# Step 1 of a convolution-and-GELU kernel: taking the first needed sum and its copy ahead of the middle channel group

## The chip, the cores and the metric

The kernel runs on one core of one Trainium2 chip. The metric is the device time of one launch in microseconds, the median of the runs shown. TensorE (PE in the profile) multiplies matrices, VectorE (DVE), ScalarE (ACT) and GpSimd (POOL) work on elements, and SyncE (SP) issues most of the DMA transfers from an in-order queue.

## The reference

```python
# x: (8, 4096, 192), weight: (8 heads, 7 taps); w_in: (192, 2048), w_out: (2048, 192)
w = softmax(weight, axis=-1)
out[b, s, h, :] = sum_k w[h, k] * x_pad[b, s + k, h, :]     # causal, 6 zeros ahead of s = 0
h = out.reshape(32768, 192) @ w_in                          # float32
g = h * sigmoid(1.702 * h)
y = g @ w_out
```

A depthwise causal convolution over 7 positions feeds a two-layer network whose hidden layer has 2048 columns. All is float32.

## The kernel before, in words

The 32768 tokens are taken in 32 steps (`big` 0 to 31). A step covers two halves of tokens at a time, and its input is turned so that channels lie on partitions. The 192 channels are three groups (`c` = 0, 1, 2) of 64, and each group gives two blocks of 256 positions: group 0 gives C11 and C12, group 1 gives C21 and C22, group 2 gives C31 and C32. A convolution of one group is seven instructions over 512 elements: the first tap is a multiplication (line 490), the other six are multiply-and-add on DVE (line 492). In step 1 the multiplication is on ACT (`times = act.mul`), in the later steps the group 0 taps run on ACT and POOL.

From step 1 on, the first matrix product is not done block by block: it uses 21 products (`TERMS`) of sums of blocks (`SUMS_C`, V1 to V8) with sums of weight blocks (`SUMS_W`). V1 is C31 - C11, so it needs groups 2 and 0 and nothing of group 1; V2 to V8 follow from it and the other blocks. A product (`product1`, line 570) runs on two halves of the partitions, and one half of each needs the block moved to the other 64 partitions. That is `cross`: two SP DMAs (line 514) from the step's own slab of `conv_t` into its middle slab. It is called three times a step: for V1 alone (2 x 64 KB), for C11 to C22 (2 x 256 KB), and for the remaining eight blocks (2 x 512 KB), V4 among them.

The order of DVE's work around the change is written as a list of (label, cost, action), made by `prepare`. `work(us)` takes actions off the front of that list as long as their costs fit the given time; `need(label)` takes all up to the label at once. `cross_when` issues a copy at once if the space that it writes is given free, and in step 1 it is free by the time that the list gets there.

Step 0 does its second matrix product in `second_first` (PE lines 739 and 745), four 32-column products at a time. While PE is in it, DVE does that stage's sums (lines 755 to 778) and the list of step 1 through `work(1.5)`, `work(5.0)`, `work(4.0)`. Then `fetch()`, which is `between` for this step, empties the list (`need("all 1")`), turns the input of step 2 (line 469), and issues step 1's first product, `terms(1, 0, slots[2], 16)`, which is V1 with a weight block. PE goes on with line 739 for the rest of step 0 and ends it with `rows22`; then `hidden(1, 0)` begins step 1 with `pe(sums, 12)`, V4 with a weight block, and `pe(x, 5, 17)`, C11 and C21.

```python
        work(4.0)
        go(c12, listed(s4, b22) + rows12[:cut], first=False)
        fetch()
        go(c21, listed(a22, b21), first=False)
        work(3.0)
        turn(1, 0, blocks(whole(c21)), js)
```

`add_forms` lets POOL issue accumulating DMAs (line 437, 240 KB each) that make sums of the second layer's weights at the same time.

Of the kernel before, what the change touches and what calls it, by code (L numbers as in the profile page):

```python
# [15 lines left out]
def kernel(  # L16
# [32 lines left out]
    H, K = weight.shape  # L49
# [31 lines left out]
    vec, act = nc.vector, nc.scalar  # L81
# [91 lines left out]
    def place(big, b):  # L173

        if b == V1:
            return V8 if big % 2 else C31
        return C31 if b == V8 and big % 2 else b

    def own(big):
        return conv_t[:, big % 2 * 2, :, :]  # L180
# [301 lines left out]
    def conv_src(big, c, k, ns=slice(0, 2)):  # L482
        return xts[big][:, c, ns, Q - PAD + k : Q - PAD + k + T]

    def conv(big, c, k, ns=slice(0, 2), times=vec.tensor_scalar_mul):
        src = conv_src(big, c, k, ns)
        dst = own(big)[:, 2 * c + ns.start : 2 * c + ns.stop, :]
        tap = cw[:, c, k : k + 1]
        if k == 0:
            times(dst, src, tap)  # L490
        else:
            vec.scalar_tensor_tensor(  # L492
                out=dst, in0=src, scalar=tap, in1=dst, op0=ALU.mult, op1=ALU.add
            )
# [10 lines left out]
    def sums_c(big, i):  # L505
        add_up(
            lambda j: own(big)[:, place(big, j), :],
            *SUMS_C[i],
            eng=vec if big == 1 else nc.gpsimd,
        )  # L510

    def cross(big, b0, b1):
        for o in range(2):
            nc.sync.dma_start(
                out=conv_t[halves[1 - o], 1, b0:b1, :], in_=own(big)[halves[o], b0:b1, :]
            )
# [11 lines left out]
    def cross_when(early, *what):  # L528
        if given[early] < what[0] - 1:
            waiting[early].append(what)  # L530
        else:
            cross(*what)
# [7 lines left out]
    def prepare(big):  # L540

        v1 = place(big, V1)
        for c in (2, 1, 0) if big == 1 else (2, 1):
            for k in range(K):
                times = act.mul if big == 1 else vec.tensor_scalar_mul
                yield "", 0.76 if k else 0.48, lambda c=c, k=k, times=times: conv(big, c, k, times=times)
        yield f"done {big}", 0.0, lambda: need(f"taps {big}")
        cost = 0.34 if big == 1 else 0.0
        yield "", cost, lambda: sums_c(big, 0)
        yield f"first {big}", 0.0, lambda: cross_when(True, big, v1, v1 + 1)  # L550
        yield "", 0.0, lambda: cross_when(False, big, 0, C31)
        for i in range(1, len(SUMS_C)):
            yield "", cost, lambda i=i: sums_c(big, i)
        rest = (C31, V8) if big % 2 else (C31 + 1, NB)
        yield f"all {big}", 0.0, lambda: cross_when(False, big, *rest)
# [430 lines left out]
    def need(label):  # L986
        for q in (todo, ready):
            while any(item[0] == label for item in q):
                q.pop(0)[2]()
# [30 lines left out]
    def first_step(fetch):  # L1020
# [81 lines left out]
        def stage_2():  # L1102
            round_w_out(0)
            load_w_out(3)
            todo.append(("", 2.1, lambda: turn_x(1)))
            todo.extend(prepare(1))
# [23 lines left out]
        def between():  # L1130
            need("all 1")
            turn_x(2)
            todo.extend(prepare(2))
            todo.append(("forms", 0.0, lambda: begin_forms(TURN_O)))
            fetch()
# [10 lines left out]
    def begin(big):  # L1146
        todo.extend(prepare(big))
        ready.extend(prepare_taps(big))
# [54 lines left out]
```

## Time and profile before

| what | value |
|---|---|
| median of 3 runs | 2319.04 us (2319.0 to 2319.4) |
| the profiled execution's own time | 2319.26 us |
| its span, first to last instruction | 2317.5 us |
| PE busy | 2306.4 us (100% of the span) |
| DVE, ACT, POOL busy | 2006.3 us, 1377.4 us, 432.8 us |
| chain that ended last, by engine | PE 98%, DVE 1% |
| PE line 570, products of the first layer into `slot` | 3740 matmuls, 590 ns each |
| `conv_t` to `conv_t` DMAs of 64 KB, median from issue to landing | 4.5 us |

The span leaves out 1.76 us of the profiled execution's own time. PE is busy nearly throughout, and its matmuls are pipelined, so that a start-to-start distance (0.43 us for a row of four products here) tells more than a duration. The time line names what an engine waited for in brackets.

### The profile page before, as it was taken

The page shows a single profiled execution, that of the slowest core. Times are in us where ns is not written, and L with a number is a line of the kernel's source. Part 1 is how long each engine was busy: PE and PEld are TensorE (multiplying, and loading weights), DVE is VectorE, ACT ScalarE, POOL GpSimd, SP SyncE. Part 2 cuts the span into 40 slices and gives each one's busy share as a digit, 9 for nine tenths or more (in the row PEclk, how much of TensorE's full clock was granted, in tenths as well). Part 3 has the DMA queues.
Part 4 walks back from the last instruction along what each step waited for, and adds up shares of the span by engine and source line. Part 5 has one row for each costly group of instructions (what it writes and reads, how often), then busy time and mean ns, then how long its engine had stood idle before and what let it go on. Part 6 is the DMA issues. An engine that isn't in the chain of part 4 may idle for free.

```text
span 2317.5 us, 60312 instructions
## 1 busy us (share of the span) xinstructions
PE 2306.4 (100%) x25982; PEld 1227.1 (53%) x25982; DVE 2006.3 (87%) x2816; ACT 1377.4 (59%) x2555; POOL 432.8 (19%) x451
## 2 busy tenths in 40 slices
PE   9999999999999999999999999999999999999999
PEld 5355555555555655555555555555555555555556
DVE  8898889888898888988888988889888898888877
ACT  7465665556655656555666555665566655556644
POOL 0311222112221022210222211222102221022200
PEclk9999999999999999999999999999999999999999
DMA  8623321223222233112331122321223321231010
GB/s 185 120 57 70 70 43 42 64 62 70 53 48 55 57 70 69 43 43 57 70 70 43 43 64 62 70 50 46 59 57 70 66 47 43 57 70 44 17 43 16
DMA packets 199867, 137.99 MB, mean 60 GB/s; under 512 B 108976, under 2 KB 190512, under 8 KB 195632
## 3 DMA queue, kind: packets, MB, share of 16 engines
q1 hardware_dynamic: 197040, 130.98, 25.6%
q0 software_dynamic: 1728, 2.95, 0.7%
q8 instruction: 204, 3.34, 0.6%
q14 instruction: 63, 0.52, 0.1%
q10 hardware_dynamic: 832, 0.20, 0.0%
HBM read 53.15 MB, written 25.17 MB: 34 GB/s over the span
## 4 chain that ended last, share of the span: by engine, by line
PE 98%; DVE 1%; DMA 0%; ACT 0%; SPq 0%; issue 0%; ACTq 0%; DVEq 0%
PE slot L570 35%; PE slot L860 33%; PE sums L570 16%; PE sums L860 14%; PE slot L739 1%; DMA osbs<-in_moe_w_in_dram 0%; DMA conv_t<-conv_t 0%; DVE conv_t L492 0%; SPq L99 0%; DVE g L774 0%; DVE osbs L812 0%; ACT conv_t L1018 0%; ACT conv_t L490 0%; ACT conv_t L350 0%; ACT conv_t L349 0%
## 5 line engine op out<-in xcount | busy, mean ns | idle before, releaser
L570 PE MATMUL slot<-conv_t,w_in_s 64*128 64x512 f32 x3740 | 853.6, 590 | 3.1 <-DMA conv_t<-conv_t 2.5
L860 PE MATMUL slot<-g,w_form 128*32 128x256 f32 x6700 | 772.5, 379 | 0.0
L570 PEld LDWEIGHTS slot<-conv_t,w_in_s 64*128 64x128 f32 x3740 | 374.3, 187 | 429.6 <-issue 383.3
L503 POOL TENSOR_TENSOR conv_t<-conv_t,g 128x512 f32<-128x512 f32 x180 | 245.3, 1363 | 1453.1 <-ACT conv_t L499 1441.4
L860 PEld LDWEIGHTS slot<-g,w_form 128*32 128x32 f32 x6700 | 399.6, 110 | 134.9 <-ACT g L591 22.0
L860 PE MATMUL sums<-g,w_form 128*32 128x256 f32 x3530 | 461.8, 379 | 0.0
L860 PE MATMUL slot<-g,w_out_s 128*32 128x256 f32 x4432 | 442.0, 379 | 0.0
L570 PE MATMUL sums<-conv_t,w_in_s 64*128 64x512 f32 x1660 | 406.7, 591 | 0.4 <-DVE w_in_s L369 0.4
L593 ACT ACTIVATE g<-room 128x1024 f32<-128x1024 f32 x310 | 324.5, 1073 | 90.9 <-DVE room L604 90.9
L492 DVE SCALAR_TENSOR_TENSOR conv_t<-xt,cw,conv_t 128x512 f32<-128x512 f32 (+1 forms) x390 | 310.5, 796 | 10.7 <-ACT conv_t L490 3.8
L860 PEld LDWEIGHTS slot<-g,w_out_s 128*32 128x32 f32 x4432 | 226.0, 110 | 97.5
L860 PEld LDWEIGHTS sums<-g,w_form 128*32 128x32 f32 x3530 | 233.3, 110 | 65.7
L570 PEld LDWEIGHTS sums<-conv_t,w_in_s 64*128 64x128 f32 x1660 | 169.6, 187 | 185.7 <-issue 149.7
L600 ACT COPY room<-slot 128x512 f32<-128x512 f32 x434 | 231.8, 602 | 57.5 <-PE slot L570 57.2
L591 ACT ACTIVATE g<-slot 128x512 f32<-128x512 f32 x334 | 179.7, 590 | 88.9 <-PE slot L570 88.9
L874 ACT COPY room<-slot 32x256 f32<-32x256 f32 x245 | 89.8, 367 | 206.1 <-PE slot L860 200.7
L860 PE MATMUL sums<-g,w_out_s 128*32 128x256 f32 x1706 | 205.3, 379 | 0.0
L860 PE MATMUL slot<-room,w_form 128*32 128x256 f32 x2340 | 182.1, 379 | 0.0
L604 DVE TENSOR_TENSOR room<-slot,room 128x512 f32<-128x512 f32 x248 | 156.3, 682 | 19.9 <-ACT room L600 19.9
L604 DVE TENSOR_TENSOR room<-room,sums 128x512 f32<-128x512 f32 x124 | 79.1, 679 | 69.0 <-PE sums L570 69.0
L604 DVE TENSOR_TENSOR room<-room,slot 128x512 f32<-128x512 f32 x124 | 79.1, 678 | 64.4 <-PE slot L570 64.4
L600 ACT COPY room<-sums 128x512 f32<-128x512 f32 x186 | 100.0, 592 | 58.2 <-PE sums L570 58.0
(211 smaller groups left out, 2668.7 us busy)
## 6 DMA issues: line engine op xcount, KB each, us to landing
xin<-in_x_dram SPq DMA_DIRECT2D x240, 180.0 KB, 4.3
conv_t<-conv_t SPq DMA_DIRECT2D x62, 512.0 KB, 4.7
out_dram<-osbs SPq DMA_DIRECT2D x186, 128.0 KB, 2.6
conv_t<-conv_t SPq DMA_DIRECT2D x62, 256.0 KB, 3.6
conv_t<-conv_t SPq DMA_DIRECT2D x62, 64.0 KB, 4.5
xin<-in_x_dram SPq DMA_DIRECT2D x16, 160.0 KB, 2.9
w_form<-w_out_s POOLq DMA_DIRECT2D x7, 240.0 KB, 4.1
osbs<-in_moe_w_out_dram SPq DMA_DIRECT2D x2, 768.0 KB, 7.6
```

The costliest lines, as they stand in the source:

```text
L492: vec.scalar_tensor_tensor(out=dst, in0=src, scalar=tap, in1=dst, op0=ALU.mult, op1=ALU.add)
L503: nc.gpsimd.tensor_add(dst, dst, tap_home(big, k))
L570: nc.tensor.matmul(slot[h], w_in_s[halves[h], a, v * P : (v + 1) * P], src, start=first, stop=True, skip_group_check=True,)
L591: act.activation(g[:, n, i + h, :], src[h], AF.Gelu_apprx_sigmoid)
L593: act.activation(g[:, n, i : i + 2, :], src, AF.Gelu_apprx_sigmoid)
L600: act.copy(bank(dst, h), bank(src, h))
L604: op(*(bank(t, h) for t in (dst, a, b)))
L739: nc.tensor.matmul(chunk(bank, c), w[:, chunk_cols(c)], t, start=first and i == 0, stop=not more and i == len(steps) - 1, skip_group_check ...
L860: nc.tensor.matmul(dst, w, t, start=first, stop=last, skip_group_check=True)
L874: act.copy(to, d)
```

## The change

In step 1 the list is made in the order group 2, group 0, then V1 and its copy, then group 1, then the copy of C11 to C22 and the remaining sums. Before, it was group 2, group 1, group 0, then V1 and its copy. The steps from 2 on keep their order. No instruction is added or taken away.

On DVE, between line 767 and V2: before, the last three additions of group 1, six of group 0, V1, V2; after, the last three additions of group 0, V1, six of group 1, V2. The stage's own sums (lines 772 to 778 of the kernel before) stay among them, now after two additions of group 1 where three of group 0 stood. ACT's two multiplications for groups 1 and 0 change places. SP's queue has the same transfers in the same order. The copy of C11 to C22 now also waits for DVE in its own right.

```diff
-        for c in (2, 1, 0) if big == 1 else (2, 1):
-            for k in range(K):
-                times = act.mul if big == 1 else vec.tensor_scalar_mul
-                yield "", 0.76 if k else 0.48, lambda c=c, k=k, times=times: conv(big, c, k, times=times)
+        def convs(*cs):
+            times = act.mul if big == 1 else vec.tensor_scalar_mul
+            for c in cs:
+                for k in range(K):
+                    yield "", 0.76 if k else 0.48, lambda c=c, k=k: conv(big, c, k, times=times)
+
+        cost = 0.34 if big == 1 else 0.0
+        yield from convs(2, 0) if big == 1 else convs(2, 1)
         yield f"done {big}", 0.0, lambda: need(f"taps {big}")
-        cost = 0.34 if big == 1 else 0.0
         yield "", cost, lambda: sums_c(big, 0)
         yield f"first {big}", 0.0, lambda: cross_when(True, big, v1, v1 + 1)
+        if big == 1:
+            yield from convs(1)
         yield "", 0.0, lambda: cross_when(False, big, 0, C31)
         for i in range(1, len(SUMS_C)):
             yield "", cost, lambda i=i: sums_c(big, i)
```

## The prediction

> **What bounds the kernel now.** The page first: its chain that ended last is PE's by 98%, and PE is busy throughout, so only what PE waits for, or what slows its clock, can move the end. The view of waits, for PE alone, lists all of that (us in total, times, longest):
>
> ```profile
> PE slot L570 <- DMA conv_t<-conv_t: 2.5, 1, 2.5
> PE sums L451 <- POOL osbs masks.py:199: 1.4, 1, 1.4
> PE slot L570 <- DVE w_in_s L369: 0.6, 1, 0.6
> PE slot L1004 <- ACT g L996: 0.5, 1, 0.5
> PE sums L570 <- DVE w_in_s L369: 0.4, 1, 0.4
> ```
>
> Five waits, 5.4 us in 2317.5; the largest is for a conv_t copy. PE's time line finds it (start, us, idle before):
>
> ```profile
> 83.83 0.61 PE L739 MATMUL slot<-g,w_out_s 128*32 128x512 f32 x3
> ...
> 86.97 1.54 PE L570 MATMUL slot<-conv_t,w_in_s 64*128 64x512 f32 x4 [2.53 <-DMA conv_t<-conv_t]
> ...
> 88.44 1.07 PE L739 MATMUL slot<-g,w_out_s 128*32 128x512 f32 x3
> ...
> 90.99 0.60 PE L739 MATMUL slot<-g,w_out_s 128*32 128x512 f32 x3
> ```
>
> This is step 1's first product, inside step 0's second. After it the rows start 0.85 us apart until 90.99, against 0.43 us before. The windows, which I cut at the edges of that slow stretch, say why (length, PE busy, granted clock, DMA share, GB/s):
>
> ```profile
> 84.44:86.97 2.53, 0.00 (x1) 1.00 1.08 211
> 86.97:87.57 0.60, 0.60 (x4) 1.00 1.03 171
> 87.57:90.98 3.41, 3.41 (x16) 0.50 1.10 267
> ```
>
> The clock is halved for 3.41 us from 87.57, just after the idle stretch, and whole again later. So the wait has a second bill.
>
> DVE's time line shows why the copy is late, and the view of line 514 from 60 to 110 us how long the copies take:
>
> ```profile
> 69.29 2.32 DVE L492 SCALAR_TENSOR_TENSOR conv_t<-xt,cw,conv_t 128x512 f32<-128x512 f32 x3
> 71.86 2.33 DVE L492 SCALAR_TENSOR_TENSOR conv_t<-xt,cw,conv_t 128x512 f32<-128x512 f32 x3 [0.25 <-ACT conv_t L490]
> ...
> 78.34 2.31 DVE L492 SCALAR_TENSOR_TENSOR conv_t<-xt,cw,conv_t 128x512 f32<-128x512 f32 x3
> 80.69 0.89 DVE L388 TENSOR_TENSOR conv_t<-conv_t 128x256 f32<-128x256 f32 x2
> ```
> ```profile
> L514 SPq DMA_DIRECT2D conv_t<-conv_t x6: 535/1272/1908, 81.1 to 87.1; - x6
> DMA to landing us min/median/max: 3.6/6.8/9.8
> ```
>
> Group 0 is finished at 80.65, V1 at 81.11, its copy is issued at 81.14 and 81.72 and lands at 86.83 (5.11 us after the second issue in the chain). PE stood ready from 84.4.
>
> **The change, step by step.**
>
> V1 moves. The three additions at 69.29 become the last of group 0. They end at 71.61; V1 takes 0.42 and ends at 72.07, 9.0 us earlier. SP has nothing to issue between 47 and 81 us, so the copy goes out at 72.1. The nearest row for its length is its own 5.7 us (81.14 to 86.83), taken beside accumulating DMAs as it would be here (POOL issues three at 71.1 to 73.8); that gives 77.8. PE asks at 84.4: 6.6 us to spare, so even twice the row would do. What else the product needs is ready: slot's last reader on ACT (line 747) ends at 77.36. This wait goes whole.
>
> What it is worth on PE: without a wait, the product follows the row of 83.83 as `pe(sums, 12)` follows the row at 99.58, after 0.53: 84.36. Its four matmuls take 0.96 there (100.11 to 101.07), and the switch back to line 739 another 0.10 (55.91 against 54.52 and three times 0.43): 85.42. The next rows come after 0.45 (55.91 to 56.36), 0.43 and 0.43: 86.73 for the row that is now at 90.99. Gain 4.26 us. The other way round: 2.53 of waiting and half of 3.41 make 4.24.
>
> Here a rule speaks against half of that: the Trainium skill, "TensorE: Matmul & The Clock Gate", section "Why this matters for your kernels", warns only of idle gaps over about 3 us as costing the clock. This gap is 2.53 us and the row shows 0.50 right behind it; the row decides. By the rule the halving would have another cause and stay, and the gain would be 2.55 us.
>
> DVE moves. It issues the same instructions. V1's 0.42 takes up the 0.25 that DVE waited at 71.86 for ACT's multiplication (ready at 71.83, V1 ends later). Two additions of group 1 follow, then the stage's sums from 73.7 instead of 74.22, with line 778 held at 77.4 by ACT's copy; then four additions instead of three (ending about 81.1), and V2 at 81.1 against 81.15. V8 ends at 83.9, as now (83.96). The stage's sums that PE reads come 0.3 to 0.5 earlier, so nobody waits longer. Cost nothing; if the cover of ACT's copy were gone it would be some tenths of DVE, which has 4.84 us idle at 88.5.
>
> SP moves. V1's two issues leave 81.14 to 83.1, so the C11 to C22 copies go out at 81.2 instead of 83.2 and the eight-block copies when V8 is there, about 83.95 instead of 85.11. The loads of x and the stores of step 0 stay behind them and come earlier too.
>
> What is late next. After the gain PE reaches `pe(sums, 12)` at 100.11 - 4.26 = 95.85, and that needs the second eight-block copy, issued at 87.07, landing 9.8 us later, at 96.87. Today 3.2 us to spare; after the change it is a wait. Its bounds: if the copy does not come earlier at all, PE starts 0.14 after it (as 86.97 follows 86.83) at 97.01, a wait of 1.16. If it comes earlier by the 1.16 us of its earlier issue, 95.71, there is none. The DMA engines are full then (share about 1 from 84 to 100), so I go by work: V1's 0.13 MB leave the stretch, at 211 GB/s 0.62 us, landing 96.25, a wait of 0.54. I take the middle of 0 and 0.54, 0.3, since both apply in part. It should not halve the clock: the early waits of 0.6 and 0.4 did not.
>
> The other followers go along with PE: DVE's `turn` at 93.37 waits for PE, ACT's copy at 92.59 too, and ACT's and DVE's work up to 101.6 hangs on these. The weight sums on DVE begin early and go on after that turn; they would end at about 94.6, before 95.85. From there on PE has no wait in this profile.
>
> Sum: 4.26 - 0.3 = 3.96. The profiled execution's own 2319.26 becomes 2315.3; it lies 0.22 above the median, so against 2319.04 it is 2315.1. The bounds 4.26 and 3.10 give 2314.8 and 2315.9. A time of no change is told from a changed one at about 0.2%, 4.64 us, so even the whole wait stays a little within.
>
> **The rivals.**
>
> The stall is dearer in the timed runs than in the profile: the edge of the slow stretch against the wait is seen once. If a second stretch of 3.41 us at half clock followed in them, the gain would be 4.26 + 1.71 = 5.97, 2313.1; a wait 0.4 us longer is enough to pass 0.2%. Against it: the profiled run is not faster than the timed ones, and they agree within 0.4 us.
>
> The eight-block copy takes the wait's place with its own half-clock stretch: 1.16 + 1.71 = 2.87 lost of 4.26, gain 1.4, 2317.6. For it: it is now 1.0 us late. Against: the wait is less than half of the one that did it.
>
> The same copy, slower: C11 to C22 now meet the accumulating DMAs from their start (they end at about 89), and the eight blocks queue behind. This decides the sign once the copy lands after 98.3 (2.55 of waiting with 1.71 of half clock use up 4.26), and loses 0.2% after 102.9, 6.0 us later than now; at 104 it is 1.1 us more, 2324.8. Against: no byte is added, and the issues come earlier.
>
> The change does not do what it says: another condition of the product is the real last one. Then PE would still start at 86.97, 2319.0. Against: the chain goes through the copy, and ACT's and DVE's parts of it end by 81.1.
>
> **How the numbers follow.** Forecast 0.50 (2314.8 to 2315.9, all within 0.2%). Dearer stall 0.28, faster. Copy with half clock 0.06 and no effect 0.04, both same. Copy so late that it loses 0.12, slower. So faster 0.28, same 0.60, slower 0.12. Most weight is near 4 us, close to the edge, which is why the dearer stall gets more than the profile argues for. The range, 2313.6 to 2317.0: below, it takes in most of the dearer stall; above, the forecast's bound and part of the half-clock case; no effect and the loss are left out.
>
> **What would show it.** Right: no wait of PE for conv_t before line 570 near 84.4, the clock at 1.00 from 87 to 91, V1 near 71.7 on DVE, a wait under 0.6 us near 95.9 with the eight-block copy landing near 96. Wrong: the clock halved again around 95 to 99; a new PE wait on DVE between 85 and 95; the copy of V1 landing after 84.

## The result, and the profile after

The changed kernel takes 2314.95 us (median of 20 runs, 2314.55 to 2316.07), against 2318.38 us for the kernel before beside it (20 runs, 2317.52 to 2319.84). The ratio is 0.9985, interval 0.9978 to 0.9992: 0.15% faster, within the 0.2% that the prediction takes for the edge of a change. The median of before lies between two groups of its own runs, ten at 2317.5 to 2318.0 and ten at 2318.8 to 2319.8; the experiments show what parts them. The profiled execution of the changed kernel took 2315.61 us with a span of 2313.9 us.

PE's waits in it (us in total, times, longest; lines are five higher than before):

```profile
PE sums L451 <- POOL osbs masks.py:199: 1.4, 1, 1.4
PE slot L1009 <- ACT g L1001: 1.0, 1, 1.0
PE sums L575 <- DMA xin<-in_x_dram: 0.6, 1, 0.6
PE slot L575 <- DVE w_in_s L369: 0.5, 1, 0.5
PE sums L575 <- DVE w_in_s L369: 0.4, 1, 0.4
```

The wait of 2.5 us for the copy is gone, and one of 0.6 us is new. PE's time line around step 1's first product, and at the start of step 1:

```profile
83.98 0.60 PE L744 MATMUL slot<-g,w_out_s 128*32 128x512 f32 x3
...
84.53 1.13 PE L575 MATMUL slot<-conv_t,w_in_s 64*128 64x512 f32 x4
85.58 0.63 PE L744 MATMUL slot<-g,w_out_s 128*32 128x512 f32 x3
...
86.90 0.60 PE L744 MATMUL slot<-g,w_out_s 128*32 128x512 f32 x3
...
96.69 1.22 PE L575 MATMUL sums<-conv_t,w_in_s 64*128 64x512 f32 x4 [0.60 <-DMA xin<-in_x_dram]
```

The product follows the row of 83.98 after 0.55 us, and the row that stood at 90.99 is at 86.90: 4.09 earlier, and 4.24 if one takes off that this execution was 0.15 later already at 83.98. Step 1 begins at 96.69 instead of 100.11. The windows over the same stretches as before show the other half (length, PE busy, clock, DMA share, GB/s):

```profile
84.44:86.97 2.53, 2.53 (x24) 1.00 1.05 201
87.57:90.98 3.41, 3.41 (x36) 1.00 1.07 211
```

PE is busy in the first, and the second has 36 matmuls at full clock where 16 ran at half. DVE's and SP's time lines:

```profile
71.79 0.42 DVE L388 TENSOR_TENSOR conv_t<-conv_t 128x256 f32<-128x256 f32 x1
```
```profile
72.24 14.33 SPq L514 DMA_DIRECT2D conv_t<-conv_t  x6
86.66 10.11 SPq L99 DMA_DIRECT2D xin<-in_x_dram  x8
```

V1 is done at 72.21 and its copy goes out at 72.24. By the trace's completion records it has landed at 76.68, 4.4 us after the first issue, beside three accumulating DMAs that POOL issued from 71.3 on. SP finishes the copies 2.3 us earlier than before and the loads of x follow at 86.66 instead of 88.92.

### The profile page after: what moved, and what is told of

It reads as the page before. It is cut to its first block, busy times and chain, and to the rows that moved or that the text cites. A ratio compares the mean times of both kernels' runs of the same rounds, so it can differ in the third digit from the quotient of the medians.

```text
span 2313.9 us, 60313 instructions
## 1 busy us (share of the span) xinstructions
PE 2304.5 (100%) x25982; PEld 1233.4 (53%) x25982; DVE 2005.2 (87%) x2816; ACT 1378.2 (60%) x2555; POOL 433.1 (19%) x451
## 4 chain that ended last, share of the span: by engine, by line
PE 98%; DVE 1%; DMA 0%; ACT 0%; issue 0%; POOL 0%; DVEq 0%; ACTq 0%; POOLq 0%
PE slot L575 35%; PE slot L865 33%; PE sums L575 16%; PE sums L865 14%; PE slot L744 1%; DMA xin<-in_x_dram 0%; DVE conv_t L492 0%; PE slot L1009 0%; PE sums L451 0%; ACT conv_t L1023 0%; DVE xt L469 0%; DVE conv_t L388 0%; ACT conv_t L1021 0%; PE slot L455 0%; ACT conv_t L350 0%
```

## The experiments

The theory: PE's idle wait for V1's copy is what the change takes away; the wait costs its own length, and halves the clock for 3.41 us besides. The rivals: DVE's order brings the gain, the copy's length is the matter, or the halving has another cause.

**When the sum is done.** `sum_late` keeps the new order of groups and puts the sum back:

```diff
+        if big == 1:
+            yield from convs(1)
         yield "", cost, lambda: sums_c(big, 0)
         yield f"first {big}", 0.0, lambda: cross_when(True, big, v1, v1 + 1)
-        if big == 1:
-            yield from convs(1)
```

> The changed kernel's order of channel groups (2, 0, 1), but the V1 sum and its copy after group 1, where they stood before. Theory (when the V1 sum is done sets when its copy is issued, and the order of the groups alone does nothing): sum near 81, copy issued near 81.2, landing near 87, a PE wait of 2.3 to 2.8 us, and the runs in the same two groups as before, 2317 to 2319.8. Rival (the order of the groups itself, through DVE's and ACT's work, brings the gain): 2315.

2317.55 us (11 runs, 2316.96 to 2319.27). PE waits 2.21 us:

```profile
86.94 1.13 PE L575 MATMUL slot<-conv_t,w_in_s 64*128 64x512 f32 x4 [2.21 <-DVE w_in_s L388]
```

The runs fall in the two groups, six at 2316.96 to 2317.55 and five at 2318.73 to 2319.27. Their medians, 2317.30 and 2318.83, are about 0.4 us under those of all runs of before (2317.75 and 2319.26, below), so the order of the channel groups alone brings some tenths at most.

**When the copy is issued.** `copy_late` was meant to hold the copy back by listing it after group 1:

```diff
-        yield f"first {big}", 0.0, lambda: cross_when(True, big, v1, v1 + 1)
         if big == 1:
             yield from convs(1)
+        yield f"first {big}", 0.0, lambda: cross_when(True, big, v1, v1 + 1)
```

> The changed kernel, with the V1 sum early but its copy issued only after group 1, ahead of the copy of C11 to C22. Theory (the place of the copy in time is all that counts): issued near 81.3, landing near 86.9, PE waits 2.3 to 2.7 us again, time as before, 2317.5 to 2319.8. Rival (the gain comes from DVE's order itself, the sum being early or the smaller wait for ACT): 2315 as in the changed kernel.

2314.90 us (11 runs), as the changed kernel, and the time line says why:

```profile
72.31 14.38 SPq L514 DMA_DIRECT2D conv_t<-conv_t  x6
```

The copy still went out at 72.31. The list orders each engine's instructions; SP had nothing ahead of the copy, and its wait is for the V1 sum alone. So this tells nothing between the theories, but that the copy's place in the list is no part of the change. `copy_behind` holds it back in earnest: on SP it stands behind the copy of C11 to C22, which waits for group 1.

```diff
-        yield f"first {big}", 0.0, lambda: cross_when(True, big, v1, v1 + 1)
         if big == 1:
             yield from convs(1)
+            yield "", 0.0, lambda: cross_when(False, big, 0, C31)
+        yield f"first {big}", 0.0, lambda: cross_when(True, big, v1, v1 + 1)
-        yield "", 0.0, lambda: cross_when(False, big, 0, C31)
+        if big > 1:
+            yield "", 0.0, lambda: cross_when(False, big, 0, C31)
```

> The changed kernel with the V1 sum early, but its copy queued on SP behind the copy of C11 to C22, which waits for group 1. Theory (the landing of the copy decides, not the sum): copy issued near 83.5, landing at 88 to 90, a PE wait of 4 to 5.5 us and at least one stretch of half clock: 2320.5 to 2323.5, slower than both kernels. Rival (the early sum brings the gain, the copy has room): 2315 to 2316.

2323.62 us (10 runs, 2322.83 to 2324.08), a little over the expected range, since the copy, issued at 83.20, landed only at 91.02 and the wait was longer. PE's time line and its windows:

```profile
91.16 2.08 PE L577 MATMUL slot<-conv_t,w_in_s 64*128 64x512 f32 x4 [6.73 <-DMA conv_t<-conv_t]
```
```profile
88.23:91.16 2.93, 0.00 (x1) 0.50 1.09 256
91.16:95.05 3.89, 3.89 (x16) 0.50 1.02 219
95.05:99.00 3.95, 3.95 (x44) 1.00 1.18 221
```

The sum was as early as in the changed kernel (71.63 on DVE); the copy was not, and all is lost. The price adds up: 6.73 of waiting and half of the 3.89 us of work at half clock, 1.95, make 8.68; 2314.95 and 8.68 are 2323.6.

**What the idle wait does to the clock.** `fill_wait` is the kernel before with two product pairs for PE to do while it waits, `fill_one` the same with one:

```diff
         need(f"first {big}")
+        for _ in range(2 if big == 1 and not v else 0):
+            for h in range(2):
+                nc.tensor.matmul(
+                    slot[h], w_in_s[halves[h], 2, 0:P], own(0)[halves[h], C11:C21, :],
+                    start=True, stop=True, skip_group_check=True,
+                )
         terms(big, v, slot, 16, first=True)
```

> The kernel before, with two extra product pairs on PE (results overwritten) ahead of step 1's first product, so that PE works through most of its wait for the copy. Theory (the idle wait halves the clock, which costs 1.7 us on top): the extra pairs take 1.72 us of the wait, 0.7 to 0.9 us of idle is left, the clock stays at 1.00 after it, and the time is 2317.5 to 2317.9 in all runs, the lower of the two groups into which the runs of before fall (2317.5 to 2318.0 and 2318.8 to 2319.8). Rival (the halving has another cause, such as the full DMA engines or the kind of product): half clock after the product as before, and the runs in two groups again.

2317.62 us, all 11 runs at 2317.22 to 2317.94. PE's time line:

```profile
84.25 1.99 PE L1155 MATMUL slot<-conv_t,w_in_s 64*128 64x512 f32 x8
87.03 1.13 PE L570 MATMUL slot<-conv_t,w_in_s 64*128 64x512 f32 x4 [0.80 <-DVE w_in_s L388]
88.09 0.63 PE L739 MATMUL slot<-g,w_out_s 128*32 128x512 f32 x3
```
```profile
87.03:91.00 3.97, 3.96 (x32) 1.00 1.06 255
```

The product starts at 87.03, no earlier than before, and the DMA engines are as busy as before (share 1.06), yet the rows after it run at full clock and only the lower group of times is left. Work that is thrown away takes 1.6 us off the upper group (2319.26 to 2317.62). The releaser that the line names, as in `sum_late`, cannot be meant. In the changed kernel the same product runs at 84.53, before the first of these weight sums of line 388 starts at 86.32. And PE starts 0.13 us after the copy's last completion record here (86.90) and 0.14 after it in `sum_late` (86.80), as it does in the kernel before, where the copy is named.

> The kernel before with one extra product pair on PE (0.86 us) ahead of step 1's first product, which leaves an idle wait of 1.5 to 1.8 us. It asks how long an idle wait must be to halve the clock. If what counts is the idle share of one stretch of 3.41 us and half of it is too little: clock at 1.00, all runs at 2317.4 to 2317.9. If any wait of over 1 us does it when it falls within one stretch: two groups of runs again, up to 2319.8.

2317.56 us. Ten runs at 2317.32 to 2318.11, one at 2319.82; the profiled one waits 1.59 us without half clock. That profile alone says little: a grid line of the clock (shown below) stands at 86.49 in it and cuts the wait into 1.12 and 0.47. The count says more. If the grid falls anywhere with equal chance, a wait of 1.6 us lies whole in one stretch of 3.41 us in about half of the runs (an estimate), but only one of eleven has the longer time. So 1.6 us of idle in one stretch is mostly too little.

Two more profiles of the kernel before, unchanged:

> The kernel before, unchanged, profiled again. Theory (the clock is decided in a fixed grid of 3.41 us, and the lower group of runs is that in which the idle wait is cut by a grid line): a run near 2317.7 shows the same 2.5 us wait, no half clock, and a grid line (counted from the clock's start near 5 us) well inside 84.4 to 87; a run near 2319.4 shows half clock and the wait within one grid stretch. Rival (the lower group has a shorter wait): a run near 2317.7 has a wait near 0.8 us.

> The kernel before, profiled a third time. The same as for the second: with a wait of 2.2 to 3.2 us, half clock and 2318.8 to 2319.8 if over 2.4 us of it lie in one grid stretch of 3.41 us, no half clock and 2317.0 to 2318.0 if a grid line cuts it into pieces of under 2 us. Rival: half clock follows the length of the wait alone.

2319.65 and 2319.22 us, both of the upper group, with waits of 3.23 and 2.66 us. The clock records have a grid of 3.41 us, counted from where the clock first rises (at 6.26 and 5.06): in every profile the stretches at one clock, but for the last, are whole multiples of 3.413 us (81.92 us at full clock ahead of the halving is 24 of them). Windows cut along it, of the second profile of before, and of `sum_late` (7.52), whose profiled run, at 2317.55, is one of the lower group:

```profile
81.35:84.76 3.41, 2.84 (x28) 1.00 1.09 193
84.76:88.18 3.42, 0.76 (x4) 1.00 1.05 199
88.18:91.59 3.41, 3.41 (x18) 0.50 1.06 275
```
```profile
82.62:86.03 3.41, 2.11 (x20) 1.00 1.08 191
86.03:89.44 3.41, 2.50 (x20) 1.00 1.07 236
89.44:92.86 3.42, 3.42 (x40) 1.00 1.03 241
```

In the first, 2.66 us of the wait lie in one grid stretch, and the stretch after it has half the clock. In `sum_late` a grid line at 86.03 cuts the wait into 1.30 and 0.91, and the clock stays. The third profile of before has 2.58 us in one stretch and half clock. The recorded rival, that half clock follows the length of the wait alone, is not excluded by these profiles, since `sum_late`'s wait of 2.21 us is also shorter than every wait that halved the clock (2.53 us and more). The times speak against it. Over the changed kernel's 2314.95, the upper group's median of 2319.26 leaves 2.60 us of wait once 1.71 of half clock is taken off, and the lower group's 2317.75 leaves 2.80, so the waits of the lower group are no shorter. The two groups are thus, by these numbers, one wait, cut by the grid or not. That a lower-group run of the unchanged kernel looks like this is inferred: no profile here is of such a run, and `sum_late` stands in for it.

**Why the copy took so long.** `before_adds_later` and `adds_later` leave the order of before, and of the changed kernel, and move the second five accumulating DMAs to the end of `second_first`:

```diff
         begin_forms(BEGIN_2)
-        add_forms(ADD_2)
...
         store(0, 1)
+        add_forms(ADD_2)
```

> The kernel before with the same five accumulating DMAs issued near 108 us. Theory (V1's copy took 5.7 us from issue to landing because the engines were full of them): the copy takes 2 to 3.5 us, lands at 83.5 to 84.8, and PE's wait shrinks to 0 to 0.5 us with no half clock: 2314.8 to 2315.6 without any reordering. Rival (the copy's length is its own): the wait stays at 2.5 us, 2317.5 to 2319.8.

2315.00 us (11 runs, 2314.68 to 2315.30): the whole gain without any reordering. The copy was issued at 80.98 and 81.57, and PE did not wait for it:

```profile
84.22 1.13 PE L570 MATMUL slot<-conv_t,w_in_s 64*128 64x512 f32 x4
```

So the late sum and the accumulating DMAs were both needed for the wait. V1's copy of 2 x 64 KB took 5.7 us in the kernel before, beside accumulating DMAs of 240 KB and with the DMA engines full (mean share 1.09 from 81.14 to 86.83). In `before_adds_later` it took 2.6 us, with its last completion record at 83.56 and a mean share of 0.44 from 80.98 to 84.22. The early copy of the changed kernel, beside three accumulating DMAs, took 4.4 us at a share of 1.00, with time to spare.

> The changed kernel, with the second five accumulating DMAs (of 240 KB) issued by POOL after step 2's tap additions, near 108 us instead of 78 to 84. Theory (the eight-block copy lands at 96.4 because those DMAs share the engines with it): it lands 2 to 3 us earlier, the wait of 0.6 us at 96 goes, time 0.3 to 0.6 under the changed kernel's, 2314.3 to 2314.7. Rival (the loads of x or the copy's own length set its landing): landing at 96 as now, the wait stays, 2315. A third: POOL's sums for step 2 now come 7 us later behind the issues; if they were on the path, over 2315.5.

2314.89 us (11 runs, 2314.78 to 2315.03). From issue to landing, the six copies of the changed kernel (first line) and of `adds_later` (second):

```profile
DMA to landing us min/median/max: 2.9/7.2/11.7
```
```profile
DMA to landing us min/median/max: 3.0/4.5/6.4
```

The last one landed at 91.0 instead of 96.4, more than expected, and the wait at 96 is gone. The median moved by 0.06, less than expected; what went is the upper end, 2315.03 against 2316.07. POOL's late sums cost nothing.

**The new wait of 0.6 us.** `c11_first` takes the products with C11 and C21 ahead of that with V4, in step 1 alone:

```diff
+        if big == 1 and not v:
+            pe(x, 5, 17)
         pe(sums, 12)
         copy2(k15, sums)
-        pe(x, 5, 17)
+        if big > 1 or v:
+            pe(x, 5, 17)
```

> The changed kernel with the first two products of step 1 taken in the other order: those with C11 and C21 (1.72 us of PE) ahead of that with V4, which needs the second eight-block copy. Theory (the 0.6 us wait near 96 in the profile of the changed kernel is for that copy, landing 95.8 to 96.5, and comes in some runs only): no wait of over 0.1 us there in any profile, PE at line 575 from 96.0, median 0 to 0.2 us lower (2314.7 to 2314.95) and no runs over 2315.3. Rival (the wait is for a load of x, as the page names it, landing at 97.0): PE still waits near 96, median and spread as in the changed kernel (2314.55 to 2316.1).

2315.01 us (11 runs, 2314.87 to 2315.43). There is no wait near 96 in the profile, but no gain either, against 0 to 0.2 us expected, and one run is over 2315.3.

`loads_later` takes the loads of x out of the stretch:

```diff
         second_first(between)
+        load_x(3)
...
-        if big + 1 < N_BIG:
+        if big + 1 < N_BIG and big != 2:
             load_x(big + 1)
```

> The changed kernel with the eight loads of x for step 3 queued after step 0's last stores, so that none is under way before 97. Theory (the copy is slow because of the accumulating DMAs ahead of it, and the loads only queue behind it): the second eight-block copy lands at 95.3 to 96.5 as before, and a wait of up to 0.7 us stays in some runs: 2314.5 to 2316. Rival (the loads hold PE up, or slow the copy): the copy lands before 95, no wait, no runs over 2315.3.

2314.80 us (11 runs, 2314.58 to 2315.21). The last copy landed at 95.1 and PE did not wait, nearer to the rival than to the theory, though in reach of both. Of 31 runs with the changed kernel's instructions (with `copy_late`'s, which builds the same queues), five are over 2315.3, so the wait seems to come in some runs only: the profile of `copy_late` (2315.03) has none, with the last copy landing at 95.77. In the profile that has it (2315.61), the last copy lands at 96.45 and PE starts at 96.69, before the first load of x lands at 97.05; so the load that the page names is not what PE waited for. Whether the loads slow that copy stays open.

## Why the prediction was right, step by step

- V1's move: forecast done at 72.07, copy out at 72.1; measured 72.21 and 72.24. That the wait goes whole held, with `sum_late` and `copy_behind` to show that sum and copy are the cause. The copy's own length was mis-sized: 5.7 us was taken, its own late row, and 4.4 was measured. With 6.6 us to spare this cost nothing.
- The worth on PE: forecast 4.26, measured 4.24 in the profile. That the halving of the clock belongs to the wait was shown by `fill_wait`. The rule of the Trainium skill that was weighed against it there ("TensorE: Matmul & The Clock Gate", section "Why this matters for your kernels", idle gaps over about 3 us) lost: gaps of 2.53 and 2.66 us were enough, and of a gap of 3.23 us 2.66 lay in one stretch.
- DVE's and SP's moves: V2 at 81.17 (forecast 81.1), copies of C11 to C22 at 81.40 (81.2), the eight-block copies from 84.04 (83.95). No new wait of PE on DVE.
- What is late next: the right copy was named, landing at 96.45 where 95.7 to 96.9 was forecast, and the wait was 0.60 where the value taken was 0.3 and the bounds 0 and 1.16. Most runs seem to have none, which the median of 2314.95 agrees with: 2319.26 less 4.26 is 2315.0.
- The rivals. A dearer stall in the timed runs: the reverse holds. In 28 of the 101 runs of before that were made beside the changed kernel and the experiments, the time is under 2318.5 (median 2317.75), the stall without its half clock. The three runs shown at first were all of the upper group (median of the 73 others 2319.26), so the sum against 2319.04 gave 2315.1 rightly. That the profile and these three runs were all of one group was luck: in a run of the lower group the same change is worth about 2.8 us (2317.75 against 2314.95), near the wait alone. So the measured change against a median of before is 3.4 instead of 4.0. The eight-block copy with a half clock of its own did not come: 0.6 us of idle did not halve anything. That copy so late that it loses did not come either; `copy_behind` shows what such lateness costs, there for V1's copy. That another condition of the product was the real one is out: it ran at 84.53 without a wait.

What the forecast did not see is that the accumulating DMAs, and not only the late sum, set the wait. It priced the early copy by the slow row, which was on the safe side.

## What to carry to other kernels

Where one engine is busy throughout, list all of its waits, look at the granted clock behind each, and price the clock with the wait. Before reordering for an early transfer, ask what else fills the DMA engines in that stretch; moving transfers that nobody needs yet gave the same gain here. After such a wait goes, the next transfer's slack shrinks by the gain: here from 3.2 us to nothing.

## What the runs showed of the hardware

A TensorE idle stretch of 2.53 to 2.66 us inside one grid stretch of 3.41 us halved the clock for the next one (three profiles of before), 1.71 us on top of the wait; 1.30 and 0.91 on two sides of a grid line did not (`sum_late`), nor did 1.12 and 0.47 (`fill_one`) or 0.80 (`fill_wait`). The Trainium skill, "TensorE: Matmul & The Clock Gate", section "What's actually happening", says that the clock is judged in windows of 3413 ns that run freely; the profiles agree, with 3.41 us, and with a start between 4.4 and 7.5 us into the span. If the grid falls anywhere with equal chance against a wait of 2.5 us, 73 of 101 runs of before in the upper group put the limit at about 1.75 us of idle in one stretch. This is a rough estimate from these counts alone, since the waits in the profiles run from 2.2 to 3.2 us and the share differs between the four sets of runs, from 10 of 20 to 18 of 21: the whole wait lies inside one stretch in 0.27 of cases, and its longer piece exceeds the limit in a further 2 x (2.5 - 1.75) / 3.41 = 0.44.
